# Operands of a B attention job loaded in halves of four heads, five steps ahead of their use

## The chip, the core and the metric

The kernel runs on one core of a Trainium2 chip. Its engines are TensorE (PE, with its weight loads shown as PEld), VectorE (DVE), ScalarE (ACT), GpSimd (POOL) and SyncE (SP), which in this kernel issues every DMA. Each engine works through its own list of instructions in order and waits on semaphores. The metric is the device time of one execution in microseconds (us), taken as the median of several runs; the profile is one more execution, recorded by the hardware.

## What is computed

Two attention blocks over the same 2048 x 512 input are mixed by a gate. Block A goes through 64 segments of 32 tokens in order; each segment attends to itself and to 8 memory rows, and its output gives the memory of the next segment. Block B has 32 heads of width 16 and four blocks of 512 tokens; inside a block it is causal softmax attention, and from the second block on a linear-attention memory of the earlier blocks is added.

```python
# A, segment s: h = [mem, x_s]; 32 heads of 128
q, k, v = h @ Wq, h @ Wk, h @ Wv
p = softmax(q k^T * 128**-0.5 + mask);  o = (p v) @ Wo
mem = o[:8];  outs.append(o[8:])
# B, block s of 512 tokens, 32 heads of 16
p = softmax(qs ks^T * 16**-0.5 + causal);  a_dot = p vs
a_mem = (phi(qs) M) / (phi(qs) z + 1e-6)
o = g * a_mem + (1 - g) * a_dot
M += phi(ks)^T vs;  z += sum(phi(ks))
out = gate * A + (1 - gate) * (B @ wo)
```

## The kernel before, in words

**Recording.** `build` records operations engine by engine through `Prog.op` and `Prog.dma`. Each names what it reads and writes, and from that the waits are derived: an operation waits for the last writer of what it reads, and one that overwrites something waits for all its readers. `emit` writes the lists out in the recorded order, so the place of a call in the Python code is the place of its instructions on each engine. All DMAs of this part stand on SP's one list, in order.

**First stage (to about 90 us).** The projections of B are computed and stored to scratch memory in HBM (`kTd`, `qTd`, `vd`, `pQd`, `mzd`), while the weights of A are loaded.

**Main stage.** `plan_a` goes through the 64 segments of A. For each it runs the units of `A_ORDER` (L822): projections K, Q, V (L855), transposes (L864), scores (S), sums (M), normalising (N), P V (PV), output product (W, L1115) and the memory for the next segment (WT, L1136). Work of B is put between as filler: `bS` and `bP` are one step of B's scores and of B's P V each, `bT` runs one piece of what is waiting in the list `late`. In a segment `bS` stands three times: at its start, and twice near its end, with W1 and one filler between these two. Some 57 of the 64 segments carry steps of B.

**Jobs, halves, steps of B.** A job is 8 heads of one block; there are 16. Step n belongs to job n // 10, to half G = (n // 5) % 2 (four heads) and to k = n % 5. Half G uses partitions 64 G to 64 G + 63 of `KTj` and `QTj`, and the 68 columns from 68 G of `Vj` and `MZj`. In the trace the five steps of a half differ by their shapes on L704: 512 columns x2 for k = 0 and 1, the 384 and 128 columns x4 for k = 2 and 3, 256 columns x4 for k = 4.

**The operands.** There is one buffer of each operand. `load(job, "k")` issues nine DMAs: eight 16-row pieces of `KTj` and one of `QTj`. `load(job, "v")` issues one of `Vj` and, from the second block on (12 of the 16 jobs), one each of `pQj` and `MZj`. The load "k" of the next job is recorded at the end of the tenth `bS` of a job (L708), and waits until that `bS` has read the buffers. The next `bS` (k = 0 of the next job) waits for this load. The load "v" of the next job is recorded in `chain` for G = 1 (L786), after the last P V of the job and after `bN`, which is the product of `pQj` and `MZj` (L779). If `bP` of a new job comes before that, it runs the waiting pieces first (L734).

**What `chain` and `finish` do.** `chain` divides by the softmax sum and adds the memory part, for one half; `finish` transposes the 8 heads' rows (`bT`, L812), and stores them.

Of the kernel before, what the change touches and what calls it, by code (L numbers as in the profile page):

```python
# [216 lines left out]
def bass_gated_mix__memory_aug_recurrent_mem_tr__memory_aug_infini_attn__prompt_kernel(  # L217
    nc, A_x, A_mem0, A_Wq, A_Wk, A_Wv, A_Wo, A_seg_len, B_x, B_wq, B_wk, B_wv, B_wo, B_beta, gate_w, out, dbg=None,
):
    with ExitStack() as es:  # L220
        build(nc, es, A_x, A_mem0, A_Wq, A_Wk, A_Wv, A_Wo, B_wq, B_wk, B_wv, B_wo, B_beta, gate_w, out, dbg)


def build(nc, es, A_x, A_mem0, A_Wq, A_Wk, A_Wv, A_Wo, B_wq, B_wk, B_wv, B_wo, B_beta, gate_w, out, dbg=None):
    v = NS()
# [83 lines left out]
    G = {}  # L309
# [19 lines left out]
    bat = v.bat = BAttn(v)  # L329
# [11 lines left out]
    while len(weights) > 4:  # L341
        weights.pop(0)()
    for part in "kv":
        bat.load(0, part)
    while weights:
        weights.pop(0)()

# [291 lines left out]
class BAttn:  # L639
# [11 lines left out]
        self.obk = None  # L651
        self.jobs_done = 0

    def load(self, job, part):

        v, P, Rs = self.v, self.v.P, self.v.Rs
        if job >= 16 or (job, part) in self.loaded:
            return
        self.loaded.add((job, part))
        sb, f = job // 4, job % 4  # L660
        g, res = P.group("j%s%d" % (part, job), "j" + part), Rs("j" + part.upper())

        def ld(dst, src, reads, name):
            P.dma(g, lambda s: s.dma_start(dst, src), reads=reads, writes=[res], name=name, scratch=True)  # L664
        if part == "k":
            for e in range(2):
                for t in range(4):
                    o = 32 * t + 16 * e
                    ld(v.KTj[e][o:o + 16, :], v.kTd[sb, f, o:o + 16, :], [Rs("kTd%d_%d" % (sb, f)), Rs("KTz")], "ldk%d_%d%d" % (job, e, t))
            ld(v.QTj[:, :], v.qTd[sb, f], [Rs("qTd%d_%d" % (sb, f))], "ldq%d" % job)  # L670
            return
        ld(v.Vj[:, :, :], v.vd[sb, :, :, 136 * f:136 * (f + 1)], [Rs("vd%d_%d" % (sb, tt)) for tt in range(4)], "ldv%d" % job)
        if sb > 0:
            ld(v.pQj[:, :], v.pQd[sb, f], [Rs("pQd%d_%d" % (sb, f))], "ldp%d" % job)
            ld(v.MZj[:, :], v.mzd[sb, :, 136 * f:136 * (f + 1)], [Rs("mzd%d" % sb)], "ldm%d" % job)

    def scores(self):
        v, P, Rs = self.v, self.v.P, self.v.Rs
        n = self.n
        self.n += 1  # L680
        job, G, k = n // 10, (n // 5) % 2, n % 5
        self.load(job, "k")
        bks = v.BK.pair()
        if k < 2:
            mms = [(k, 0, 0, 512, 0)]
            blocks = [(k, 0, q, 128 * q) for q in range(4)]
            diag = [0]
        elif k < 4:
            mms = [(k - 2, 1, 128, 384, 0), (k - 2, 3, 384, 128, 384)]
            blocks = [(k - 2, 1, q, 128 * (q - 1)) for q in (1, 2, 3)] + [(k - 2, 3, 3, 384)]  # L690
            diag = [0, 384]
        else:
            mms = [(e, 2, 256, 256, 256 * e) for e in range(2)]
            blocks = [(e, 2, q, 256 * e + 128 * (q - 2)) for e in range(2) for q in (2, 3)]
            diag = [0, 256]
        self.blocks[n] = blocks
        QT, KT = v.QTj, v.KTj

        def f(pe):
            ins = None  # L700
            for e, kc, q0, w, o in mms:
                for x in range(2):
                    r = slice(64 * G + 32 * x, 64 * G + 32 * x + 32)
                    ins = pe.matmul(v.pb[bks[x]][:, o:o + w], KT[e][r, 128 * kc:128 * (kc + 1)], QT[r, q0:q0 + w], start=True, stop=True,  # L704
                                    tile_position=(r.start, 0))
            return ins
        P.op("pe", f, reads=[Rs("jK")], writes=[v.rbank[b] for b in bks], name="bS%d" % n)
        if n % 10 == 9:  # L708
            self.load(job + 1, "k")
        pt = v.PT[n % 2]  # L710
        rp = Rs("PT%d" % (n % 2))
        P.op("act", lambda a: a.activation(pt[:, :, :], v.ps[:, bks[0]:bks[1] + 1, :], ACT.Exp, scale=v.SCALE_B),  # L712
             reads=[v.rbank[b] for b in bks], writes=[rp], name="bE%d" % n)
        v.BK.give(*bks)
        if k == 4:
            views = [pt[:, :, :].rearrange("p x (d t) -> p (x d) t", t=256)[:, :, 0:128]]
        else:
            views = [pt[:, :, o:o + 128] for o in diag]
        for mv in views:
            P.op("gp", lambda g, mv=mv: g.affine_select(mv, mv, [[0, mv.shape[1]], [1, 128]], ALU.is_ge, 0.0, base=0, channel_multiplier=-1),  # L720
                 reads=[rp], writes=[rp], name="bM%d" % n)
# [6 lines left out]
    def pv(self):  # L728
        v, P, Rs = self.v, self.v.P, self.v.Rs
        n = self.pv_n  # L730
        self.pv_n += 1
        job, G, k = n // 10, (n // 5) % 2, n % 5
        sb, f = job // 4, job % 4
        while self.late and (job, "v") not in self.loaded:  # L734
            self.run_late(1)
        self.load(job, "v")
        if k == 0:
            self.obk = v.BK.take(long=True)
        ob = self.obk
        pt, V = v.PT[n % 2], v.Vj  # L740
        blocks = self.blocks.pop(n)

        def fpv(pe):
            ins = None
            first = k == 0
            for e, kc, q, col in blocks:
                for x in range(2):
                    hh = 2 * x + e
                    o = 17 * (4 * q + hh)
                    h = 4 * G + hh  # L750
                    ins = pe.matmul(v.pb[ob][:, o:o + 17], pt[:, x, col:col + 128], V[:, kc, 17 * h:17 * (h + 1)], start=first, stop=True,  # L751
                                    skip_group_check=True)
                    first = False
            return ins
        P.op("pe", fpv, reads=[Rs("PT%d" % (n % 2)), Rs("jV")], writes=[v.rbank[ob]], name="bP%d" % n)
        if k == 4:
            self.late.append(lambda: self.chain(job, G, ob))
            if G == 1:
                self.late.append(lambda: self.finish(sb, f))

    def chain(self, job, G, ob):
        v, P, Rs = self.v, self.v.P, self.v.Rs
        sb, f = job // 4, job % 4
        h0 = 8 * f + 4 * G
        nm = "%d_%d%d" % (sb, f, G)
        T1 = v.pb[ob][:, 0:272].rearrange("p (q h w) -> p q h w", q=4, h=4)
        dst = v.orow[:, :, 64 * G:64 * (G + 1)].rearrange("p q (h d) -> p q h d", h=4)
# [4 lines left out]
        nb = None  # L772
        if sb:
            nb = v.BK.take()

            def fn(pe):
                ins = None
                for q in range(4):
                    ins = pe.matmul(v.pb[nb][:, 68 * q:68 * (q + 1)], v.pQj[:, 128 * q:128 * (q + 1)], v.MZj[:, 68 * G:68 * (G + 1)],  # L779
                                    start=True, stop=True)  # L780
                return ins
            P.op("pe", fn, reads=[Rs("jV")], writes=[v.rbank[nb]], name="bN" + nm)
            T2 = v.pb[nb][:, 0:272].rearrange("p (q h w) -> p q h w", q=4, h=4)
        P.op("dve", lambda d: d.reciprocal(rd, T1[:, :, :, 16]), reads=[v.rbank[ob], rr], writes=[rr], name="brd" + nm)
        P.op("dve", lambda d: d.tensor_tensor(rd, rd, bc(v.omgB_sb), ALU.mult), reads=[rr, Rs("omgB")], writes=[rr], name="brg" + nm)
        if G == 1:  # L786
            self.load(job + 1, "v")
        if not sb:
            P.op("dve", lambda d: d.tensor_tensor(dst, T1[:, :, :, 0:16], up(rd), ALU.mult), reads=[v.rbank[ob], rr], writes=[ro], name="bo" + nm)
            v.BK.give(ob)  # L790
# [38 lines left out]
def plan_a(v, nseg):  # L829
# [163 lines left out]
    def segment(s, fill):  # L993
# [179 lines left out]
        for b in range(2):  # L1173
            for m in "KQV":
                units["%s%d" % (m, b)] = lambda m=m, b=b: nat_pass(m, b, ENG["%s%d" % (m, b)])
            for m in "KQ":
                units["T%s%d" % (m, b)] = lambda m=m, b=b: tr(m, b, ENG["T%s%d" % (m, b)])
            units["S%d" % b] = lambda b=b: scores(b)
            units["M%d" % b] = lambda b=b: sums(b)
            units["N%d" % b] = lambda b=b: norm(b)  # L1180
            units["PV%d" % b] = lambda b=b: held.__setitem__(b, pv(b))
            units["W%d" % b] = lambda b=b: wo(b)
            for half in range(2):
                units["E%d%s" % (b, "ab"[half])] = lambda b=b, half=half: out_ev(b, half)
# [74 lines left out]
```

## Time and profile before

| what | value |
|---|---|
| median of 3 runs | 1195.66 us |
| the profiled execution, its time | 1193.82 us |
| its span, first to last instruction | 1192.1 us (1.7 us of its time lie around the span) |
| PE busy | 1026.2 us (86%) |
| ACT busy | 671.2 us (56%) |
| DVE busy | 513.3 us (43%) |
| POOL busy | 212.5 us (18%) |
| mean granted clock of TensorE | 0.959 of full speed |

Busy time is an average over stages; waits are read from the views that say what ended them. The granted clock is 1.00 (2.4 GHz) or 0.50 (1.2 GHz) at any moment, a window shows the mean.

### The profile page before, as it was taken

What the parts mean: (1) busy time and instruction counts of PE and PEld (TensorE: products, weight loads), DVE (VectorE), ACT (ScalarE), POOL (GpSimd) and SP (SyncE); (2) the same over time, 40 slices, a digit from 0 to 9 for tenths busy, and PEclk for the clock granted to TensorE, in tenths of its full rate; (3) what the DMA queues carried; (4) which work ended last, traced back from release to release, by engine and by line L of the source; (5) the groups of instructions that cost most, each with busy time, mean ns of one, the idle gap of its engine ahead of it and who ended that gap; (6) DMA issues with size and microseconds to landing.
All of it is one profiled execution on the core that took longest, in us unless ns stands there. A gap on an engine that the chain in (4) does not pass through costs nothing.

```text
span 1192.1 us, 54216 instructions
## 1 busy us (share of the span) xinstructions
PE 1026.2 (86%) x24389; PEld 553.3 (46%) x24389; DVE 513.3 (43%) x1309; ACT 671.2 (56%) x1371; POOL 212.5 (18%) x544
## 2 busy tenths in 40 slices
PE   8968997899789799979998999698978899999874
PEld 4424544454445455444554555354534455554432
DVE  4643443344335444444444444243433444444432
ACT  4435665566546566656665666365645656655442
POOL 6101111111112121211122121121211121220000
PEclk9989999899989899999999999899989999999997
DMA  8894000000011101010101010000010001000001
GB/s 270 272 319 145 13 12 12 17 12 17 12 26 34 31 17 31 8 26 3 41 21 44 4 39 8 25 8 22 28 32 17 16 22 30 18 8 21 26 3 32
DMA packets 55551, 51.79 MB, mean 43 GB/s; under 512 B 23696, under 2 KB 53784, under 8 KB 53784
## 3 DMA queue, kind: packets, MB, share of 16 engines
q1 hardware_dynamic: 55320, 48.32, 13.4%
q8 instruction: 192, 3.15, 1.1%
q14 instruction: 39, 0.32, 0.1%
HBM read 33.60 MB, written 14.70 MB: 41 GB/s over the span
## 4 chain that ended last, share of the span: by engine, by line
PE 73%; ACT 9%; DVE 7%; DMA 5%; SPq 3%; issue 3%; POOL 1%; ACTq 0%; POOLq 0%; DVEq 0%
PE ps L855 35%; PE ps L1115 8%; PE ps L864 6%; PE ps L704 4%; SPq L664 3%; PE ps L751 3%; PE ps L583 2%; ACT PT L712 2%; PE ps L558 2%; DVE Pn_sb L1064 2%; PE ps L1078 2%; DMA QTj<-scr_qTd 2%; PE ps L918 2%; PE ps L964 1%; ACT R_sb L1057 1%
## 5 line engine op out<-in xcount | busy, mean ns | idle before, releaser
L712 ACT ACTIVATE PT<-ps 128x1024 bf16<-128x1024 f32 x160 | 163.3, 1022 | 99.1 <-PE ps L704 95.3
L855 PE MATMUL ps<-Wk_sb,hT 128*32 128x512 bf16 x2048 | 142.5, 401 | 0.7 <-DVE hT L1142 0.6
L720 POOL TENSOR_SCALAR_AFFINE_SELECT PT<-PT 128x256 bf16<-128x256 bf16 (+1 forms) x224 | 98.4, 439 | 223.8 <-ACT PT L712 215.3
L855 PE MATMUL ps<-Wq_sb,hT 128*32 128x512 bf16 x2048 | 137.1, 389 | 0.0
L855 PE MATMUL ps<-Wv_sb,hT 128*32 128x512 bf16 x2048 | 135.5, 383 | 1.6 <-DVE amem L801 0.9
L1115 PE MATMUL ps<-Wo_sb,OT_sb 128*32 128x512 bf16 x2048 | 134.5, 384 | 1.7 <-DMA Wo_sb<-in_A_Wo_dram 1.7
L1169 POOL COPY OTL<-OT_sb 128x256 bf16<-128x256 bf16 x64 | 25.4, 397 | 545.3 <-DVE OT_sb L321 432.9
L1125 DVE TENSOR_TENSOR aW_sb<-ps,aW_sb 128x256 bf16<-128x256 f32 x128 | 48.4, 420 | 152.3 <-ACT aW_sb L319 152.3
L319 ACT ACTIVATE KN_sb<-ps 128x512 bf16<-128x512 f32 x64 | 38.2, 597 | 128.7 <-PE ps L855 128.7
L704 PE MATMUL ps<-QTj,KTj 32*128 32x384 bf16 (+3 forms) x512 | 64.8, 310 | 41.5 <-DMA QTj<-scr_qTd 40.5
L319 ACT ACTIVATE OT_sb<-ps 128x320 bf16<-128x320 f32 x192 | 75.9, 429 | 19.6 <-PE ps L1087 19.0
L855 PEld LDWEIGHTS ps<-Wq_sb,hT 128*32 128x32 bf16 x2048 | 56.1, 100 | 60.9 <-issue 6.8
L855 PEld LDWEIGHTS ps<-Wk_sb,hT 128*32 128x32 bf16 x2048 | 50.5, 100 | 62.9 <-issue 16.0
L321 DVE CAST KN_sb<-ps 128x512 bf16<-128x512 f32 x64 | 44.2, 691 | 80.8 <-PE ps L855 80.6
L1057 ACT ACTIVATE R_sb<-ps 128x160 f32<-128x160 f32 x128 | 38.9, 304 | 69.6 <-PE ps L1053 69.6
L1078 PE MATMUL ps<-Pn_sb,V_sb 32*128 32x40 bf16 x2048 | 36.4, 178 | 44.5 <-DVE Pn_sb L1068 39.1
L751 PEld LDWEIGHTS ps<-Vj,PT 128*128 128x128 bf16 x1280 | 44.5, 96 | 55.7 <-issue 39.4
L751 PE MATMUL ps<-Vj,PT 128*128 128x17 bf16 x1280 | 57.4, 172 | 14.9 <-DMA MZj<-scr_mzd 10.6
L321 DVE COPY QT_sb<-ps 128x512 bf16<-128x512 bf16 x64 | 27.2, 425 | 99.5 <-PE ps L864 99.5
L1064 DVE TENSOR_TENSOR Pn_sb<-P_sb,R_sb 128x160 bf16<-128x160 bf16 x128 | 44.1, 345 | 51.0 <-ACT R_sb L1060 42.2
L1115 PEld LDWEIGHTS ps<-Wo_sb,OT_sb 128*32 128x32 bf16 x2048 | 43.4, 96 | 46.8 <-issue 14.9
L855 PEld LDWEIGHTS ps<-Wv_sb,hT 128*32 128x32 bf16 x2048 | 46.1, 95 | 35.0 <-ACT R_sb L1057 1.5
(136 smaller groups left out, 1827.1 us busy)
## 6 DMA issues: line engine op xcount, KB each, us to landing
Wk_sb<-in_A_Wk_dram SPq DMA_DIRECT2D x4, 1024.0 KB, 6.7
Wq_sb<-in_A_Wq_dram SPq DMA_DIRECT2D x4, 1024.0 KB, 7.0
Wv_sb<-in_A_Wv_dram SPq DMA_DIRECT2D x4, 1024.0 KB, 8.1
Wo_sb<-in_A_Wo_dram SPq DMA_DIRECT2D x4, 1024.0 KB, 11.6
scr_vd<-V SPq DMA_DIRECT2D x16, 136.0 KB, 5.1
Vj<-scr_vd SPq DMA_DIRECT2D x16, 136.0 KB, 2.7
Wo_sb<-in_A_x_dram SPq DMA_DIRECT2D x4, 512.0 KB, 8.1
scr_kTd<-stgk SPq DMA_DIRECT2D x16, 128.0 KB, 6.1
```

Of the source, the lines that this page charges most:

```text
L319: P.op("act", lambda a: a.activation(dst, src, ACT.Copy), reads=[v.rbank[k] for k in bks], writes=dres, name=name)
L321: P.op("dve", lambda d: d.tensor_copy(dst, src), reads=[v.rbank[k] for k in bks], writes=dres, name=name)
L704: ins = pe.matmul(v.pb[bks[x]][:, o:o + w], KT[e][r, 128 * kc:128 * (kc + 1)], QT[r, q0:q0 + w], start=True, stop=True, tile_position=(r.s ...
L712: P.op("act", lambda a: a.activation(pt[:, :, :], v.ps[:, bks[0]:bks[1] + 1, :], ACT.Exp, scale=v.SCALE_B), reads=[v.rbank[b] for b in bks ...
L720: P.op("gp", lambda g, mv=mv: g.affine_select(mv, mv, [[0, mv.shape[1]], [1, 128]], ALU.is_ge, 0.0, base=0, channel_multiplier=-1), reads= ...
L751: ins = pe.matmul(v.pb[ob][:, o:o + 17], pt[:, x, col:col + 128], V[:, kc, 17 * h:17 * (h + 1)], start=first, stop=True, skip_group_check= ...
L855: ins = pe.matmul(pb[bk][SEG * j:SEG * (j + 1), :], lhs(c), w_sb[:, c, n0:n0 + 512], start=(c == 0), stop=(c == C - 1))
L864: ins = pe.transpose(pb16[bk][:, i * 128:(i + 1) * 128], nat[:, b, i * 128:(i + 1) * 128], ident[:, :])
L1057: P.op("act", lambda a: a.activation(R_sb[:, b, :], pb[bk][:, 224:384], ACT.Ln), reads=[rbank[bk]], writes=[Rs("R%d" % b)], name="ln%d_%d" ...
L1064: P.op("dve", lambda d: d.tensor_tensor(wide(Pn_sb, b)[:, :, 0:L], wide(P_sb, b)[:, :, 0:L], R_sb[:, b, :].rearrange("p (i q) -> p i q", q ...
L1078: ins = pe.matmul(pb[bks[j]][:, L * i:L * (i + 1)], V_sb[SEG * j:SEG * (j + 1), b, i * E:(i + 1) * E], Pn_sb[SEG * j:SEG * (j + 1), b, LW ...
L1115: ins = pe.matmul(pb[bk][SEG * j:SEG * (j + 1), :], OT_sb[:, h, 0:SEG], Wo_sb[:, h, :], start=(b == 0 and i == 0), stop=(b == 1 and i == 3))
```

## The change

Every load is split by half: part "k" into four pieces of `KTj` and 64 rows of `QTj`, part "v" into 68 columns of `Vj` and `MZj` and 64 rows of `pQj`. Each half has its own name for dependencies (`jK0`, `jK1`, `jV0`, `jV1`), so a `bS` or `bP` waits for its half alone. The half G of the next job is recorded when the fifth step of that half of this job is recorded (k = 4), or, for part "v", in `chain` of that half. `bN` reads all 128 rows of `pQj`, so it now waits for both halves of part "v", of which one may already belong to the next job; the columns of `MZj` that it uses are zero in the other half's rows.

```diff
     for part in "kv":
-        bat.load(0, part)
+        for G in range(2):
+            bat.load(0, G, part)
...
-    def load(self, job, part):
+    def load(self, job, G, part):
...
-        g, res = P.group("j%s%d" % (part, job), "j" + part), Rs("j" + part.upper())
+        g, res = P.group("j%s%d_%d" % (part, job, G), "j%s%d" % (part, G)), Rs("j%s%d" % (part.upper(), G))
+        rows, cols = slice(64 * G, 64 * G + 64), slice(68 * G, 68 * G + 68)
...
         if part == "k":
             for e in range(2):
-                for t in range(4):
+                for t in (2 * G, 2 * G + 1):
                     o = 32 * t + 16 * e
...
-            ld(v.QTj[:, :], v.qTd[sb, f], [Rs("qTd%d_%d" % (sb, f))], "ldq%d" % job)
+            ld(v.QTj[rows, :], v.qTd[sb, f, rows, :], [Rs("qTd%d_%d" % (sb, f))], "ldq")
             return
...
+        o = 136 * f + 68 * G
+        ld(v.Vj[:, :, cols], v.vd[sb, :, :, o:o + 68], [Rs("vd%d_%d" % (sb, tt)) for tt in range(4)], "ldv")
         if sb > 0:
...
+            ld(v.pQj[rows, :], v.pQd[sb, f, rows, :], [Rs("pQd%d_%d" % (sb, f))], "ldp")
+            ld(v.MZj[:, cols], v.mzd[sb, :, o:o + 68], [Rs("mzd%d" % sb)], "ldm")
...
-        P.op("pe", f, reads=[Rs("jK")], writes=[v.rbank[b] for b in bks], name="bS%d" % n)
-        if n % 10 == 9:
-            self.load(job + 1, "k")
+        P.op("pe", f, reads=[Rs("jK%d" % G)], writes=[v.rbank[b] for b in bks], name="bS%d" % n)
+        if k == 4:
+            self.load(job + 1, G, "k")
...
-        while self.late and (job, "v") not in self.loaded:
+        while self.late and (job, G, "v") not in self.loaded:
             self.run_late(1)
-        self.load(job, "v")
+        self.load(job, G, "v")
...
-            P.op("pe", fn, reads=[Rs("jV")], writes=[v.rbank[nb]], name="bN" + nm)
+            P.op("pe", fn, reads=[Rs("jV0"), Rs("jV1")], writes=[v.rbank[nb]], name="bN" + nm)
...
-        if G == 1:
-            self.load(job + 1, "v")
+        self.load(job + 1, G, "v")
```

On SP, the loads of job 2 (the first three rows) and of job 3 stand in the kernel before with a store of finished rows of B (L817) and one of A (L945) between them:

```order
L664 DMA KTj<-scr_kTd 16x512 x8
L664 DMA QTj<-scr_qTd 128x512
L664 DMA Vj<-scr_vd 128x4x136
L817 DMA scr_oTd<-oTs 128x512
L945 DMA scr_aTd<-aT_st 128x512
L664 DMA KTj<-scr_kTd 16x512 x8
L664 DMA QTj<-scr_qTd 128x512
L664 DMA Vj<-scr_vd 128x4x136
```

In the changed kernel (its lines 667, 820 and 948 are lines 664, 817 and 945 of before) the two halves of job 2 are these, with the same two stores behind the second:

```order
L667 DMA KTj<-scr_kTd 16x512 x4
L667 DMA QTj<-scr_qTd 64x512
L667 DMA Vj<-scr_vd 128x4x68
L667 DMA KTj<-scr_kTd 16x512 x4
L667 DMA QTj<-scr_qTd 64x512
L667 DMA Vj<-scr_vd 128x4x68
L948 DMA scr_aTd<-aT_st 128x512
L820 DMA scr_oTd<-oTs 128x512
```

Each half's group of DMAs stands on SP's list where five steps of the other half of the same buffers are still to run, and the job's loads are 10 and 2 (or 6) DMAs in place of 9 and 1 (or 3).

On PE, the list of before has the transposes of a finished job, L812, directly behind the first `bP` of the next job (L751) and ahead of the scores of A, L1023, at four places (jobs 2, 4, 11 and 13; this is the first):

```order
L751 MATMUL ps<-Vj,PT 128x17 x8
L864 MATMUL ps<-ident,QN_sb 128x128 x4
L751 MATMUL ps<-Vj,PT 128x17 x8
L812 MATMUL ps<-ident,orow 128x128 x4
L1023 MATMUL ps<-mneg,ident 32x224 x4
```

In the changed kernel they stand (as L815) at the end of that segment, behind WT (L1139) and ahead of the next `bS` (L708):

```order
L1139 MATMUL ps<-selL,aW_sb 128x32 x8
L939 MATMUL ps<-selL,LN_sb 128x32 x8
L815 MATMUL ps<-ident,orow 128x128 x4
L708 MATMUL ps<-QTj,KTj 128x384 x2
```

Those four moves, two of which also move the `bN` (L779) behind the `bP` beside it, are all that moves on PE; ACT and POOL keep their order, and DVE moves the copies of the four transposes with them.

## Rows read from the trace of the kernel before

**Rows 1.** The page: span, busy time by engine, granted clock by slices.
```profile
span 1192.1 us, 54216 instructions
PE 1026.2 (86%) x24389; PEld 553.3 (46%) x24389; DVE 513.3 (43%) x1309; ACT 671.2 (56%) x1371; POOL 212.5 (18%) x544
PEclk9989999899989899999999999899989999999997
```

**Rows 2.** Groups by line: busy, mean ns | idle before, what ended it.
```profile
L704 PE MATMUL ps<-QTj,KTj 32*128 32x384 bf16 (+3 forms) x512 | 64.8, 310 | 41.5 <-DMA QTj<-scr_qTd 40.5 <-ACT PT L712 0.3
L751 PE MATMUL ps<-Vj,PT 128*128 128x17 bf16 x1280 | 57.4, 172 | 14.9 <-DMA MZj<-scr_mzd 10.6 <-DMA Vj<-scr_vd 2.6 <-POOL PT L720 1.5
```

**Rows 3.** The line of the loads (L664): who waited for it (us, times).
```profile
  PE ps L704: 40.5, 9
  PE ps L751: 13.2, 4
```

**Rows 4.** Timeline of PE, end of segment 6 to segment 7: start, us, instruction [idle <-releaser].
```profile
202.23 0.58 PE L1136 MATMUL ps<-selL,aW_sb 128*128 128x32 bf16 x8
207.93 0.61 PE L704 MATMUL ps<-QTj,KTj 32*128 32x512 bf16 x2 [5.12 <-DMA QTj<-scr_qTd]
208.47 1.90 PE L855 MATMUL ps<-Wk_sb,hT 128*32 128x512 bf16 x16
211.59 1.03 PE L855 MATMUL ps<-Wk_sb,hT 128*32 128x512 bf16 x16
...
218.43 0.36 PE L751 MATMUL ps<-Vj,PT 128*128 128x17 bf16 x8 [2.65 <-DMA Vj<-scr_vd]
```

**Rows 5.** Timeline of SP's list at the same place, and at one later load.
```profile
202.08 3.56 SPq L664 DMA_DIRECT2D KTj<-scr_kTd  x8
205.68 0.42 SPq L664 DMA_DIRECT2D QTj<-scr_qTd  x1
...
453.27 0.34 SPq L986 DMA_DIRECT2D out_dram<-aTg  x1
453.71 3.37 SPq L664 DMA_DIRECT2D KTj<-scr_kTd  x5
```

**Rows 6.** Windows with a load wait: window, us, busy by engine, PEclk, DMA.
```profile
321.60:349.30 27.70, 18.77 (x387) 9.53 (x383) 7.74 (x21) 10.44 (x22) 2.51 (x6) 0.75 0.14 36
935.60:972.50 36.90, 30.88 (x772) 17.08 (x770) 15.72 (x42) 21.13 (x43) 6.74 (x16) 0.95 0.10 25
sum 281.10, PE 213.74 PEld 112.79 DVE 101.69 ACT 134.00 POOL 41.42; mean PE 23.75 PEld 12.53 DVE 11.30 ACT 14.89 POOL 4.60
```

**Rows 7.** Windows between them, without such a wait, same columns.
```profile
110.20:202.20 92.00, 84.15 (x2218) 46.47 (x2215) 40.07 (x104) 60.38 (x123) 17.51 (x44) 1.00 0.04 9
842.90:875.90 33.00, 31.26 (x777) 16.98 (x774) 15.64 (x41) 21.71 (x45) 7.04 (x17) 1.00 0.10 27
sum 676.30, PE 627.41 PEld 345.17 DVE 309.83 ACT 439.00 POOL 136.51; mean PE 62.74 PEld 34.52 DVE 30.98 ACT 43.90 POOL 13.65
```

**Rows 8.** Windows inside segment 7: the wait, and the time after it.
```profile
204.50:211.30 6.80, 3.37 (x30) 1.21 (x34) 0.69 (x1) 1.02 (x1) 0.67 (x2) 0.50 0.14 33
211.30:218.10 6.80, 4.48 (x80) 2.25 (x72) 2.30 (x6) 2.80 (x5) 0.00 (x0) 1.00 0.10 20
218.10:221.60 3.50, 3.17 (x76) 1.98 (x80) 0.42 (x1) 0.36 (x1) 0.00 (x0) 0.51 0.12 40
```

**Rows 9.** Loads by tile: issue ns on SP, min/median/max, and time to landing (QTj, Vj).
```profile
L664 SPq DMA_DIRECT2D KTj<-scr_kTd x128: 303/420/1567, 82.3 to 1010.3; - x128
L664 SPq DMA_DIRECT2D QTj<-scr_qTd x16: 416/421/431, 86.5 to 1010.8; - x16
DMA to landing us min/median/max: 2.0/2.1/5.1
L664 SPq DMA_DIRECT2D Vj<-scr_vd x16: 529/530/612, 86.9 to 1011.8; - x16
DMA to landing us min/median/max: 2.6/2.7/5.0
```

**Rows 10.** Timeline of PE: a step k = 4, the next job's k = 0; `bN` of both halves.
```profile
123.01 0.39 PE L704 MATMUL ps<-QTj,KTj 32*128 32x256 bf16 x4
153.33 0.39 PE L704 MATMUL ps<-QTj,KTj 32*128 32x512 bf16 x2
668.09 0.29 PE L779 MATMUL ps<-MZj,pQj 128*128 128x68 bf16 x4
689.78 0.28 PE L779 MATMUL ps<-MZj,pQj 128*128 128x68 bf16 x4
```

**Rows 11.** Timeline around the first job: SP's loads, PE's wait for `Wo_sb`.
```profile
87.60 8.03 SPq L448 DMA_DIRECT2D Wo_sb<-in_A_Wo_dram  x4
104.94 1.40 PE L1115 MATMUL ps<-Wo_sb,OT_sb 128*32 128x512 bf16 x16 [1.73 <-DMA Wo_sb<-in_A_Wo_dram]
```

More of the change, by code (lines that the diff above doesn't have):

```diff
@@ L652, in __init__ @@
         self.jobs_done = 0
-    def load(self, job, part):
+    def load(self, job, G, part):
         v, P, Rs = self.v, self.v.P, self.v.Rs
-        if job >= 16 or (job, part) in self.loaded:
+        if job >= 16 or (job, G, part) in self.loaded:
             return
-        self.loaded.add((job, part))
+        self.loaded.add((job, G, part))
         sb, f = job // 4, job % 4
-        g, res = P.group("j%s%d" % (part, job), "j" + part), Rs("j" + part.upper())
+        g, res = P.group("j%s%d_%d" % (part, job, G), "j%s%d" % (part, G)), Rs("j%s%d" % (part.upper(), G))
+        rows, cols = slice(64 * G, 64 * G + 64), slice(68 * G, 68 * G + 68)
         def ld(dst, src, reads, name):
-            P.dma(g, lambda s: s.dma_start(dst, src), reads=reads, writes=[res], name=name, scratch=True)
+            P.dma(g, lambda s: s.dma_start(dst, src), reads=reads, writes=[res], name="%s%d_%d" % (name, job, G), scratch=True)
         if part == "k":
             for e in range(2):
-                for t in range(4):
+                for t in (2 * G, 2 * G + 1):
                     o = 32 * t + 16 * e
-                    ld(v.KTj[e][o:o + 16, :], v.kTd[sb, f, o:o + 16, :], [Rs("kTd%d_%d" % (sb, f)), Rs("KTz")], "ldk%d_%d%d" % (job, e, t))
-            ld(v.QTj[:, :], v.qTd[sb, f], [Rs("qTd%d_%d" % (sb, f))], "ldq%d" % job)
+                    ld(v.KTj[e][o:o + 16, :], v.kTd[sb, f, o:o + 16, :], [Rs("kTd%d_%d" % (sb, f)), Rs("KTz")], "ldk")
+            ld(v.QTj[rows, :], v.qTd[sb, f, rows, :], [Rs("qTd%d_%d" % (sb, f))], "ldq")
             return
-        ld(v.Vj[:, :, :], v.vd[sb, :, :, 136 * f:136 * (f + 1)], [Rs("vd%d_%d" % (sb, tt)) for tt in range(4)], "ldv%d" % job)
+        o = 136 * f + 68 * G
+        ld(v.Vj[:, :, cols], v.vd[sb, :, :, o:o + 68], [Rs("vd%d_%d" % (sb, tt)) for tt in range(4)], "ldv")
         if sb > 0:
-            ld(v.pQj[:, :], v.pQd[sb, f], [Rs("pQd%d_%d" % (sb, f))], "ldp%d" % job)
-            ld(v.MZj[:, :], v.mzd[sb, :, 136 * f:136 * (f + 1)], [Rs("mzd%d" % sb)], "ldm%d" % job)
+            ld(v.pQj[rows, :], v.pQd[sb, f, rows, :], [Rs("pQd%d_%d" % (sb, f))], "ldp")
+            ld(v.MZj[:, cols], v.mzd[sb, :, o:o + 68], [Rs("mzd%d" % sb)], "ldm")
     def scores(self):
@@ L681, in scores @@
         job, G, k = n // 10, (n // 5) % 2, n % 5
-        self.load(job, "k")
+        self.load(job, G, "k")
         bks = v.BK.pair()
@@ L754, in fpv @@
             return ins
-        P.op("pe", fpv, reads=[Rs("PT%d" % (n % 2)), Rs("jV")], writes=[v.rbank[ob]], name="bP%d" % n)
+        P.op("pe", fpv, reads=[Rs("PT%d" % (n % 2)), Rs("jV%d" % G)], writes=[v.rbank[ob]], name="bP%d" % n)
         if k == 4:
```

## The prediction

> **What bounds the kernel now.** I read first the page [rows 1]. PE is busy for 86% of the span, no other engine for more than 56%, so PE's own list sets the pace, and the question is when PE stands still or runs slow. The row of the clock has an 8 in six of its 40 slices where the others have a 9: something repeats that slows TensorE. The groups by line say what [rows 2]: PE stood idle 41.5 us ahead of B's scores (L704), of which 40.5 us were ended by a load of QTj, and 14.9 us ahead of B's P V (L751), of which 10.6 + 2.6 us were ended by loads of MZj and Vj. The view of line L664, from which these loads come, has the count: 9 waits of the scores and 4 of P V [rows 3]. Together 40.5 + 13.2 = **53.7 us**.
>
> The timeline shows one of the nine [rows 4, 5]. SP can start on the next job's KTj only when the tenth step has been read, at 202.08; it takes about 4 us to issue nine DMAs one after the other, the last lands 2 us later, and the next step, which stands only one P V and WT further on PE's list, waits from about 202.8 to 207.93. All of A's next segment stands behind it. In six more of the 15 changes of job a segment or its longer part lies between the two steps, and PE doesn't wait. In the same segment P V of the new job waits once more, for a load of Vj that could only be recorded just ahead of it.
>
> A wait costs more than its own length. In the 6.8 us window around its end the granted clock is 0.50, that is 1.2 GHz in place of 2.4 [rows 8]; the sixteen matmuls of a projection take 1.90 us there and 1.03 us after it [rows 4]. So I cut the main stage, from WT of segment 0 (110.2) to WT of segment 56 (1067.6), into nine stretches with such waits and the ten between them. The nine hold 13 segments and last 281.1 us, their clocks 0.75 to 0.95 [rows 6]. The ten hold 43 segments and last 676.3 us, and the clock of each is 1.00 [rows 7].
>
> **The change part by part.** *The waits and the slow time behind them.* An undisturbed segment takes 676.3 / 43 = 15.73 us. Thirteen would take 204.5 us and took 281.1: **76.6 us** are lost to load waits and what follows them. Of this 53.7 us are the waits, so 22.9 us are work at the lower clock. That this is the right size: in the nine stretches length times (1 - clock) adds up to 33 us, and some 10 of these fall into the waits themselves, where nothing runs. For the bounds I take the quickest undisturbed stretch, 92.0 / 6 = 15.33 us a segment, which gives 281.1 - 199.3 = 81.8, and the slowest, 33.0 / 2 = 16.5, which gives 66.6. I take 76.6, since the 13 segments lie at all four places in the groups of four.
>
> *Whether the halves come in time.* Part "k" of half G is now wanted six steps after the step that frees it. The closest such pair before is 123.01 to 153.33 [rows 10], 30 us. What a half takes isn't in the trace: four KTj and one QTj, by the rows of the wholes 5 x 0.42 = 2.1 us to issue [rows 9], or 5 x 0.67 = 3.4 at the slowest pace of a group that is shown [rows 5]; the landing between QTj's 2.0 and 5.1 us. That is 4.1 to 8.5 us of 30. Part "v" is closest at `bN`: half 0 of the next job is recorded right behind `bN` of half 0 and wanted by `bN` of half 1, because that reads all of pQj; 668.09 to 689.78 is 21.7 us [rows 10]. It needs three issues of about half a microsecond and a landing of at most Vj's 5.0 us [rows 9]: 6.6 us. If the cover were gone, PE would wait these 6.6 us at `bN`, A's scores of that segment stand behind it, and DVE's division behind both.
>
> *SP's list.* The DMAs of the loads go from 16 x 9 + 4 + 12 x 3 = 184 to 16 x 10 + 4 x 2 + 12 x 6 = 240. The 56 more, at 0.42 to 0.53 us each [rows 9], are 24 to 30 us on an engine that mostly waits; nothing of PE's list waits for them. A load could stand behind another entry that waits. But every such entry was recorded earlier, so what it waits for runs earlier on PE too: at 453.27 the load stood behind an output store and was let go 0.4 us after it [rows 5]. With a whole group ahead of it a half is late by 3 or 4 us, of 21.7. Cost zero.
>
> *More waits to decode.* PE has some 50 more semaphore waits, of which nearly all are met when they are reached. In the rows of L704 only 41.5 - 40.5 = 1.0 us of idle time has another cause than the loads, over all 160 steps, six met changes of job among them [rows 2]; so between 0 and 1 us. I take 0.
>
> *The four moved transposes.* They go from ahead of A's scores to behind WT, where they stand at most of the other 12 changes of job, whose segments are among the undisturbed ones. Zero, and at most the 0.6 us that one takes, either way, times four.
>
> *The first job.* Its loads stand on SP's list ahead of the four loads of Wo_sb [rows 11]. One QTj and one Vj more are 0.42 + 0.53 = 0.95 us [rows 9], and PE already waits 1.73 us for Wo_sb [rows 11]. So **1.0 us lost**; at best nothing, if not the issue but the transfer sets the landing.
>
> *A rule that speaks against it.* QTj's 128 rows landed in 2.1 us and a 16-row piece of KTj took the same 0.42 us to issue [rows 9], so I don't expect a half to be cheaper than a whole. The Trainium skill (DMA: Bandwidth & Descriptors, Rules for kernel authors) says of two transfers to disjoint partition halves "Don't bother": they share the same engines and serialize, one transfer over 128 partitions is to be preferred. By it alone the split buys nothing, and with the 24 to 30 us of issues added the time would be about 1220. The rows agree on the price and decide otherwise on the sum, since here the split moves the transfer away from its use.
>
> **The sum.** 1193.8 (the profiled execution) - 76.6 + 1.0 = 1118.2. The median of the runs is 1.8 above the profiled one, so **1120.0 us**.
>
> **The rivals.**
> *The clock doesn't come back.* If the low clock has another cause than the waits, only the idle time returns: 1195.7 - 53.7 + 1.0 = 1143. For it: nothing but its presence in single windows. Against it: it is 1.00 in all ten stretches without waits [rows 7]. 4%.
> *The halves cost as much as wholes and stay in view.* This is the mechanism behind the rule above: 10 and 6 DMAs in two portions. A whole part "k" takes about 4.0 + 2.1 = 6.1 us, two halves 2 x (2.1 + 2.1) = 8.4; 16 jobs with 2.3 us more, and half of the old wait exposed at some of them, leave about 40 us: 1160. Against it are the 30 and 21.7 us of cover. 3%.
> *The change doesn't do what it says for "k".* The loads are recorded early but SP reaches them late, behind stores that wait for work of A. Then the nine long waits stay and only the four of P V go, 13.2 us and some 6 of slow clock: 1176. For it: SP has one list. Against it: the order above, in which no entry waits for something recorded later. 2%.
> *Slower.* `bN` now depends on the next job's half. There are 24 of them, and the change loses when each waits more than 76.6 / 24 = 3.2 us; that is when a half of part "v" is let go so late that it lands 21.7 + 3.2 = 24.9 us after its record. With no cover at all, 24 x 6.6 = 158 us of new waits, 1195.7 - 76.6 + 158 = 1277. Nothing in the landing times (at most 5.1 us) speaks for it. 3%.
>
> **How the numbers follow.** The likeliest case has 88%. Its own range comes from the quickest and slowest segments and the first job: 1195.7 - 81.8 = 1113.9 to 1195.7 - 66.6 + 1.0 + 1.0 = 1131.1. I widen it below by 2 us for the transposes, and give 1112 to 1132; the rivals' 12% lie outside. A measurement of this kernel can tell about 2%, 24 us: faster below 1171.8. Likeliest case, clock and halves are faster: 95%. The rival in which "k" stays is within 2%: 2%. Slower: 3%.
>
> **What the changed profile would show.** No row of L708 or L755 (the scores and P V of the changed kernel) with idle time ended by a load; the clock 1.00 from 110 us to the end of B's steps; WT to WT never more than 17 us in that time; 240 issues on the line of the loads; the wait for Wo_sb longer by about 1 us. The argument is wrong if segments of over 20 us are left, if the clock falls without a wait ahead of it, or if `bN` (L782) waits for a DMA.

## The result and the profile after

The changed kernel takes 1120.24 us (median of 4 runs, 1118.31 to 1122.67), the kernel before 1195.41 us beside it. The ratio is 0.938, with a 95% interval of 0.935 to 0.941; it leaves out one of the four runs of the kernel before, which took 1680.55 us. Two more measurements of the same program gave 0.9386 and 0.9368. The forecast was 1120.

| what | before | after |
|---|---|---|
| median | 1195.41 us | 1120.24 us |
| span of the profiled execution | 1192.1 us | 1121.0 us |
| PE busy | 1026.2 us (86%) | 1006.3 us (90%) |
| PE idle ahead of B's scores | 41.5 us | 1.1 us |
| PE idle ahead of B's P V | 14.9 us | 1.7 us |
| mean granted clock | 0.959 | 0.983 |

The page of the changed kernel, in the lines of [rows 1]:

```profile
span 1121.0 us, 54313 instructions
PE 1006.3 (90%) x24389; PEld 547.4 (49%) x24389; DVE 511.8 (46%) x1309; ACT 670.3 (60%) x1371; POOL 212.2 (19%) x544
PEclk9988999999999999999999999999999999999997
```

PE does the same 24389 matmuls in 20 us less busy time, because fewer of them run at 1.2 GHz; the 8s in the middle of the clock row are gone. The groups by line show what became of the waits (L708 and L755 are L704 and L751 of before, the answer to [rows 2]):

```profile
L708 PE MATMUL ps<-QTj,KTj 32*128 32x384 bf16 (+3 forms) x512 | 62.9, 303 | 1.1 <-ACT PT L716 0.2
L755 PE MATMUL ps<-Vj,PT 128*128 128x17 bf16 x1280 | 57.3, 172 | 1.7 <-POOL PT L724 1.5
```

In these two rows no idle time is ended by a DMA any more. The timeline of PE at the place of [rows 4], from WT of segment 6 on (L1139):

```profile
201.84 0.58 PE L1139 MATMUL ps<-selL,aW_sb 128*128 128x32 bf16 x8
202.36 0.39 PE L708 MATMUL ps<-QTj,KTj 32*128 32x512 bf16 x2
202.71 1.05 PE L858 MATMUL ps<-Wk_sb,hT 128*32 128x512 bf16 x16
...
217.30 0.58 PE L1139 MATMUL ps<-selL,aW_sb 128*128 128x32 bf16 x8
218.30 0.35 PE L939 MATMUL ps<-selL,LN_sb 128*128 128x32 bf16 x8 [0.42 <-DVE hT L1145]
218.50 0.38 PE L815 MATMUL ps<-ident,orow 128*128 128x128 bf16 x4
```

The new job's first scores follow WT at once, the projection behind them takes 1.05 us and not 1.90, and segment 7 lasts 217.30 - 201.84 = 15.5 us, where it lasted 26.2. The transposes of the finished job stand behind WT.

A half of `QTj` or of `Vj` costs about what the whole cost, as the rows by tile show (issue on SP in ns, then landing; QTj with 64 rows, Vj with 68 columns; [rows 9] has the wholes):

```profile
L667 SPq DMA_DIRECT2D QTj<-scr_qTd x32: 450/464/1677, 81.9 to 938.0; - x32
DMA to landing us min/median/max: 2.0/2.1/6.0
L667 SPq DMA_DIRECT2D Vj<-scr_vd x32: 526/558/630, 85.0 to 940.0; - x32
DMA to landing us min/median/max: 2.3/2.5/4.3
```

### The profile page after: what moved, and what is told of

It is laid out like the page before. It is cut to its first block, busy times and chain, and to the rows that moved or that the text cites. A ratio compares the mean times of both kernels' runs of the same rounds, so it can differ in the third digit from the quotient of the medians.

```text
span 1121.0 us, 54313 instructions
## 1 busy us (share of the span) xinstructions
PE 1006.3 (90%) x24389; PEld 547.4 (49%) x24389; DVE 511.8 (46%) x1309; ACT 670.3 (60%) x1371; POOL 212.2 (19%) x544
## 4 chain that ended last, share of the span: by engine, by line
PE 76%; ACT 9%; DVE 8%; DMA 3%; issue 3%; SPq 0%; POOL 0%; ACTq 0%; DVEq 0%; POOLq 0%
PE ps L858 37%; PE ps L1118 10%; PE ps L867 6%; PE ps L708 4%; ACT PT L716 3%; PE ps L755 3%; PE ps L584 2%; DVE Pn_sb L1067 2%; PE ps L921 2%; PE ps L967 2%; PE ps L1081 2%; PE ps L559 1%; PE ps L1139 1%; DMA scr_pQd<-stgp 1%; ACT R_sb L1060 1%
## 5 line engine op out<-in xcount | busy, mean ns | idle before, releaser
L1118 PE MATMUL ps<-Wo_sb,OT_sb 128*32 128x512 bf16 x2048 | 137.3, 391 | 3.3 <-DMA Wo_sb<-in_A_Wo_dram 3.3
L858 PE MATMUL ps<-Wk_sb,hT 128*32 128x512 bf16 x2048 | 134.3, 382 | 0.8 <-DVE hT L1145 0.6
L858 PE MATMUL ps<-Wq_sb,hT 128*32 128x512 bf16 x2048 | 133.6, 381 | 0.0
L755 PEld LDWEIGHTS ps<-Vj,PT 128*128 128x128 bf16 x1280 | 44.4, 96 | 41.7 <-issue 28.4
L708 PE MATMUL ps<-QTj,KTj 32*128 32x384 bf16 (+3 forms) x512 | 62.9, 303 | 1.1 <-ACT PT L716 0.2
L319 ACT ACTIVATE V_sb<-ps 128x512 bf16<-128x512 f32 x64 | 38.2, 597 | 42.8 <-PE ps L858 42.8
```

The lines of the kernel that those rows point to most:

```text
L319: P.op("act", lambda a: a.activation(dst, src, ACT.Copy), reads=[v.rbank[k] for k in bks], writes=dres, name=name)
L858: ins = pe.matmul(pb[bk][SEG * j:SEG * (j + 1), :], lhs(c), w_sb[:, c, n0:n0 + 512], start=(c == 0), stop=(c == C - 1))
L1118: ins = pe.matmul(pb[bk][SEG * j:SEG * (j + 1), :], OT_sb[:, h, 0:SEG], Wo_sb[:, h, :], start=(b == 0 and i == 0), stop=(b == 1 and i == 3))
```

## The experiments

Seven questions were put to the chip: do the two parts add up, is it the split or the freedom to start that counts, how much lead is needed, does the slow clock come from the waits, what are the four moved transposes worth, what does the start cost, and does the first profile's odd clock repeat.

### One part at a time

Part "k" alone as changed, part "v" loaded whole as before (only the core of the diff against the changed kernel):

```diff
     def load(self, job, G, part):
+        G = 0 if part == "v" else G
...
-        self.load(job + 1, G, "v")
+        if G == 1:
+            self.load(job + 1, 0, "v")
```

> Only part 'k' (KTj, QTj) is loaded in halves and early; part 'v' is loaded whole, recorded in chain of the second half, as before. Theory (each load wait costs its length and the slow clock behind it, independently of the others): the nine waits of the scores are gone, the four of P V stay with 13.2 us of idle time and some 15 us at half clock behind them, about 7 us: 1120.2 + 20 = 1140 us. Rival (removed waits come back as longer waits elsewhere, so parts don't add up): the four waits of P V grow well beyond 13 us and the time is over 1150 us.

Measured: 1138.21 us, ratio 0.954 (0.952 to 0.956). The rows of the loads' line say who waited:

```profile
  PE ps L755: 13.5, 4
```

Four waits of P V, 13.5 us in all, each within 0.3 us of its length before. And part "v" alone, with "k" loaded whole after the tenth step:

```diff
     def load(self, job, G, part):
+        G = 0 if part == "k" else G
...
-        if k == 4:
-            self.load(job + 1, G, "k")
+        if n % 10 == 9:
+            self.load(job + 1, 0, "k")
```

> Only part 'v' (Vj, pQj, MZj) is loaded in halves and early; part 'k' is loaded whole after the tenth step, as before. Theory (costs add): nine waits of the scores stay at about 40 us, the four of P V are gone, 1195.4 - 20 = 1175 us; together with the run with 'k' alone the two gains (55 and 20) make up the 75 us. Rival (parts don't add): less than 10 us gained, because the segments that lost both waits are set by the longer one: over 1185 us.

Measured: 1178.70 us, ratio 0.987 (0.985 to 0.989). Nine waits of the scores are left:

```profile
  PE ps L708: 39.6, 9
```

By the ratios "k" is worth 55 us and "v" 16 us (13 to 18), together 71 of the 73 to 75 that both bring. The parts add, within the intervals; no wait came back elsewhere. The 20 us expected for "v" were a little too many.

### The split without the early record

```diff
-        if k == 4:
-            self.load(job + 1, G, "k")
+        if n % 10 == 9:
+            for g in range(2):
+                self.load(job + 1, g, "k")
...
-        self.load(job + 1, G, "v")
+        if G == 1:
+            for g in range(2):
+                self.load(job + 1, g, "v")
```

> The loads are split in the same halves, but both halves of the next job are recorded where the whole was before: 'k' after the tenth step, 'v' in chain of the second half. Theory (the gain is the early place, not the split): the first half needs 4 KTj and one QTj, 2.2 us of issue and 2.1 us of landing, in place of 6.1 us, so the nine waits shrink by about 1.9 us each, 17 us; the four of P V stay at about 13 us; the clock still falls: 1195.4 - 17 = 1178 us, down to 1165 if some of the shorter waits leave the clock up. Rival (smaller transfers are the gain): under 1145 us. The Trainium skill (DMA: Bandwidth & Descriptors, Rules for kernel authors) would have two transfers to disjoint halves serialize with no gain: 1195 us or more.

Measured: 1131.14 us, ratio 0.949 (0.945 to 0.952). The expectation was wrong by over 30 us, and the rival's side was right on the number but not on the reason. The timeline of SP's list has the answer:

```profile
170.38 1.70 SPq L667 DMA_DIRECT2D KTj<-scr_kTd  x4
172.12 0.48 SPq L667 DMA_DIRECT2D QTj<-scr_qTd  x1
201.27 1.69 SPq L667 DMA_DIRECT2D KTj<-scr_kTd  x4
203.00 0.47 SPq L667 DMA_DIRECT2D QTj<-scr_qTd  x1
```

The first two rows are half 0 of job 2, whose use is at 201.94. They are recorded behind the tenth step of job 1, which PE runs at 200.85, and yet they start at 170.38, right behind the last step of half 0 (169.95 on PE's timeline). The place of the record only says what stands ahead of a load on SP's list. The load starts when these entries are through and its own semaphores are met, and half 0's load names half 0 alone. For part "k", what makes the load early is the separate name more than the separate place. The place still counts for something: by the same two timelines the loads "k" of half 0 of eight jobs (5 to 9 and 13 to 15) stand behind other entries and start 18 to 34 us after their half is free, yet still 10 us or more ahead of their use.

What is left of the waits is this, on PE's timeline:

```profile
718.74 0.34 PE L756 MATMUL ps<-Vj,PT 128*128 128x17 bf16 x8 [3.51 <-DMA MZj<-scr_mzd]
835.76 0.35 PE L756 MATMUL ps<-Vj,PT 128*128 128x17 bf16 x8 [3.49 <-DMA MZj<-scr_mzd]
```

Two waits of part "v", of jobs 11 and 13, both in the blocks where `bN` exists. The load of half 0 is recorded here behind `bN` of the second half, which reads all of `pQj`, and a load waits for the readers recorded ahead of it. In the changed kernel it is recorded ahead of that `bN`. For part "v", then, the place of the record does count.

### The split, tied to the old release

To see the split without its freedom, every half load of that kernel also waits for the last operation recorded on PE:

```diff
+        last = P.ops["pe"][-1:] if job else []
...
-            P.dma(g, lambda s: s.dma_start(dst, src), reads=reads, writes=[res], name="%s%d_%d" % (name, job, G), scratch=True)
+            P.dma(g, lambda s: s.dma_start(dst, src), reads=reads, writes=[res], deps=last, name="%s%d_%d" % (name, job, G), scratch=True)
```

> The kernel of halves_late, in which every half load in addition waits for the last operation recorded on PE at that place: 'k' for the tenth step of the job, 'v' for the product bN or P V of the second half. So the transfers are split, but no half may start before the whole could. New theory (halves_late was fast because half 0 was free to start as soon as its own last reader was done, wherever its load is recorded): now the waits are back, the first half of 'k' needs 2.2 us of issue and 2.1 of landing after the tenth step in place of 6.0, nine waits of some 2.8 us, 25 us; the four of P V stay at about 13 us; 1195.4 - 16 = 1179 us, down to 1164 if the clock stays up behind the shorter waits. Rival (smaller transfers as such bring the gain): about 1131 us, as halves_late.

Measured: 1182.28 us, ratio 0.985 (0.979 to 0.991), by the ratio 1177 on the scale of 1195.4. The rows of the loads' line:

```profile
  PE ps L709: 22.8, 9
  PE ps L757: 13.1, 4
```

Nine waits of 2.5 us on average in place of 4.5 [rows 3], and the four of P V unchanged. Smaller transfers alone are worth 18 us, 11 to 26 by the interval. The other 57 need the early start, and some 8 of them also the new place of the four transposes, which this kernel has at the old one (see below). Here the Trainium skill's rule (DMA: Bandwidth & Descriptors, Rules for kernel authors), that two transfers to disjoint partition halves are not worth making because they serialize, is half borne out. On SP's timeline the issue of half 1 of job 2 does follow that of half 0 (`KTj` from 205.02 and from 207.28 us). But PE needs only half 0 to go on, and does so at 208.92 us, before `QTj` of half 1 is issued at 209.29. Whether the transfers themselves serialize isn't shown by this run.

### Half 0 freed of `bN`

If the reader decides, then the two waits left in the late version come from `bN` of the second half, which reads all of `pQj`. So it was given its own 64 rows:

```diff
-                    ins = pe.matmul(v.pb[nb][:, 68 * q:68 * (q + 1)], v.pQj[:, 128 * q:128 * (q + 1)], v.MZj[:, 68 * G:68 * (G + 1)],
-                                    start=True, stop=True)
+                    ins = pe.matmul(v.pb[nb][:, 68 * q:68 * (q + 1)], v.pQj[hr, 128 * q:128 * (q + 1)], v.MZj[hr, 68 * G:68 * (G + 1)],
+                                    start=True, stop=True, tile_position=(64 * G, 0))
...
-            P.op("pe", fn, reads=[Rs("jV0"), Rs("jV1")], writes=[v.rbank[nb]], name="bN" + nm)
+            P.op("pe", fn, reads=[Rs("jV%d" % G)], writes=[v.rbank[nb]], name="bN" + nm)
```

> The kernel of halves_late, in which bN uses only its own half's 64 rows of pQj and MZj (the other half's rows are multiplied with zeros) and waits for its own half of part 'v' alone. In halves_late two waits of 3.5 us for MZj are left, at jobs 11 and 13, with 3.4 us at half clock behind each. New theory (half 0 of part 'v' was held until bN of the second half, because that read it; the reader decides, not the place of the load): both waits are gone and the time is that of the changed kernel, 1121 us, within 2. Rival (the place of the load in chain of the second half holds it up): the two waits stay, 1131 us.

Measured: 1128.67 us, ratio 0.942 (0.939 to 0.945). No PE instruction waits for a load of B's operands any more, as the theory said, but the time didn't follow. PE's timeline at the same two places:

```profile
714.30 0.36 PE L756 MATMUL ps<-Vj,PT 128*128 128x17 bf16 x8
716.98 0.38 PE L819 MATMUL ps<-ident,orow 128*128 128x128 bf16 x4 [2.32 <-POOL orow L810]
...
832.56 0.38 PE L819 MATMUL ps<-ident,orow 128*128 128x128 bf16 x4 [2.32 <-POOL orow L810]
```

In this kernel the transposes `bT` still stand directly behind `bN` and P V, and wait for DVE and POOL to finish the rows that they transpose. That the wait for the load had hidden this one is what the next run tests.

### The four moved transposes put back

This was tested on the changed kernel itself, with all loads early and PE's list that of the kernel before:

```diff
-        while self.late and (job, G, "v") not in self.loaded:
+        while self.late and ((job, G, "v") not in self.loaded or (n % 10 == 0 and len(self.late) > 1)):
```

> The changed kernel with the four transposes (bT) put back ahead of A's scores, so that PE's list is that of the kernel before; all loads stay halved and early. Theory from late_own (the wait for the load covered the time that DVE and GpSimd need between bN and the transposes): PE waits about 2.3 us for the rows at jobs 11 and 13 and 0.6 us at jobs 2 and 4, with some 3.4 us at half clock behind the first two: 5.8 + 2 to 3 us, 1121 + 8 = 1129 us. Rival (the four moves cost and gain nothing, as predicted): 1121 us, no wait at the transposes.

Measured: 1128.07 us, ratio 0.944 (0.940 to 0.948); the changed kernel beside it took 1119.18 us, ratio 0.937 (0.933 to 0.941). PE's timeline, idle time ahead of the transposes at the four places:

```profile
213.14 0.40 PE L815 MATMUL ps<-ident,orow 128*128 128x128 bf16 x4 [0.60 <-DVE orow L792]
323.42 0.40 PE L815 MATMUL ps<-ident,orow 128*128 128x128 bf16 x4 [0.60 <-DVE orow L792]
721.48 0.38 PE L815 MATMUL ps<-ident,orow 128*128 128x128 bf16 x4 [2.53 <-POOL orow L806]
835.90 0.59 PE L815 MATMUL ps<-ident,orow 128*128 128x128 bf16 x4 [2.53 <-POOL orow L806]
```

These are 6.3 us of idle time, and behind the last one some 3.4 us at half clock. From WT of segment 0 to WT of segment 56 this kernel takes 1004.07 - 113.21 = 890.9 us, and the changed one beside it 993.38 - 110.81 = 882.6. So the move (of the transposes, and at two of the places of `bN`) is worth about 8 us, which the prediction had put at zero. In the kernel before, PE's timeline at job 11 has the wait for the load, and the transposes behind it wait for nothing:

```profile
764.72 0.36 PE L751 MATMUL ps<-Vj,PT 128*128 128x17 bf16 x8 [3.73 <-DMA MZj<-scr_mzd]
764.94 0.59 PE L812 MATMUL ps<-ident,orow 128*128 128x128 bf16 x4
```

### Two steps of lead

```diff
-        if k == 4:
-            self.load(job + 1, G, "k")
+        if k == 3 and n > 5:
+            self.load(job + G, 1 - G, "k")
```

> The changed kernel with the half loads of part 'k' recorded at step k = 3 of the other half, two steps ahead of use instead of six; part 'v' unchanged. In the changed kernel's trace the time from such a step to the use is 2.9 to 3.6 us at nine of the 30 places and over 12 us at the others. Theory (a half needs 2.2 us of issue and 2.1 us of landing, 4.3 us, and all cover beyond that is worth nothing): nine waits of about 1 us, clock mostly up, 1120 + 10 = 1130 us, up to 1140 if the clock falls behind some of them. Rival (a half needs the upper bound, 8.5 us): nine waits of about 5 us with slow clock, over 1175 us. Rival (the distance matters for another reason, such as SP's list): waits at the places with 12 us too.

Measured: 1121.53 us, ratio 0.938 (0.935 to 0.941), the same as the changed kernel beside it (0.9386). No wait for a load of B's operands is left. The expectation rested on the same error as the one for the late halves: that the place of the record is the time of the start. SP's timeline for the load "k" of half 1 of job 2, in the changed kernel (first row) and in this one:

```profile
201.69 1.70 SPq L667 DMA_DIRECT2D KTj<-scr_kTd  x4
...
222.13 0.43 SPq L820 DMA_DIRECT2D scr_oTd<-oTs  x1
222.61 2.65 SPq L667 DMA_DIRECT2D KTj<-scr_kTd  x4
```

The load does start later here, by 21 us, directly behind a store that stands ahead of it on the list; but its use is at 235.80, another 13 us later. From job 1 on, the loads "k" start 11 to 28 us ahead of their use in this kernel and 29 to 44 us ahead in the changed one, and a half needs about 4.3 (2.2 to issue and 2.1 to land). So none came late, and how little lead would do stays open.

### The waits filled with matmuls

The kernel before, with bursts of matmuls ahead of the 13 waiting operations:

```diff
+FILL_S = {20: 22, 40: 20, 50: 21, 70: 20, 90: 11, 110: 21, 120: 18, 130: 20, 140: 17}
+FILL_P = {20: 10, 40: 13, 110: 15, 130: 14}
...
+                ins = pe.matmul(v.pb[bks[0]], v.ident[:, :], v.woB_sb[:, i % 4, :], start=True, stop=True)
...
+        self.fill(FILL_S.get(n), bks)
         P.op("pe", f, reads=[Rs("jK")], writes=[v.rbank[b] for b in bks], name="bS%d" % n)
```

> The kernel before, with 128x512 matmuls into banks that are overwritten next put ahead of the 13 operations that wait for a load, as many as take up about each wait (9 bursts of 11 to 22, 4 of 10 to 15, 0.216 us each at full clock). The loads stay late. Theory (the slow clock behind a wait comes from TensorE's idle time): the clock stays at 1.00 through the main stage, the idle time is merely filled, and only the 22.9 us come back: 1172.5 us, between 1168 and 1180 if a burst is off by some tenths of a us. Rival (the clock falls for another reason, such as the transfer or the change of job): clock below 1 in the same stretches and 1195 us or more.

Measured: 1174.50 us, ratio 0.984 (0.981 to 0.987), 16 to 22 us gained with every load as late as before. PE still waits 6.2 us for the loads, in short pieces. One window over the main stage has the clock that the theory asked for, and none of its 56 segments, read one by one, has a mean below 0.99:

```profile
110.00:1050.00 940.00, 870.93 (x21370) 472.66 (x21362) 411.23 (x1080) 573.61 (x1164) 177.78 (x427) 1.00 0.08 21
```

So the slow clock came with TensorE's idle time, not with the change of job or the transfer, and it was worth about 20 us of the 75.

### The start

```diff
     for part in "kv":
-        for G in range(2):
-            bat.load(0, G, part)
+        bat.load(0, 0, part)
     while weights:
         weights.pop(0)()
+    for part in "kv":
+        bat.load(0, 1, part)
```

> The changed kernel with the second halves of job 0's loads (4 KTj, QTj, Vj) recorded behind the four loads of Wo_sb instead of ahead of them. In the changed kernel's trace these six issues take 3.0 us, and PE waits 3.3 us for Wo_sb at 103.5 us with 6.8 us at half clock from 102.9. Theory (Wo_sb lands when SP issues it): the wait is 0.3 us, and 3 to 6 us are gained: 1114 to 1117 us. Rival (the transfer of 4 MB, not the issue, sets the landing): the wait stays near 3 us and the time at 1120 us.

Measured: 1118.56 us, ratio 0.9367 (0.9339 to 0.9394), against 0.9386 (0.9358 to 0.9413) for the changed kernel beside it. The intervals overlap, so a gain isn't shown. The wait itself differs from one execution of the same program to the next: in three profiles of the changed kernel it was 3.3, 1.2 and 2.9 us, here 1.0.

```profile
L1118 PE MATMUL ps<-Wo_sb,OT_sb 128*32 128x512 bf16 x2048 | 137.3, 391 | 3.3 <-DMA Wo_sb<-in_A_Wo_dram 3.3
L1118 PE MATMUL ps<-Wo_sb,OT_sb 128*32 128x512 bf16 x2048 | 134.8, 385 | 1.2 <-DMA Wo_sb<-in_A_Wo_dram 1.2
```

(The first row is of the profile after, the second of its first repetition.) This is the only version that might beat the changed kernel, and it stays open whether it does.

### The changed kernel again

> The changed kernel once more, beside the next two on one chip. All theories: 1120 us within 2. Its first profile has two falls of the clock to 0.50, at 529.5 and 546.6 us, with no load wait ahead of them. If they belong to the place in the program, they are at the same segments (27 and 28) again; if they are a matter of chance, elsewhere or nowhere, and the main stage from WT of segment 0 to WT of segment 56 is about 4 us shorter, 882 us.

Measured: 1121.14 us. 

> The changed kernel beside it on the same chip: 1121 us within 2. A third profile of the same program shows whether the clock falls anywhere between 110 and 996 us without a wait for a load: in the first it did twice, in the second not.

Measured: 1119.18 us. In neither profile does the clock fall between 110 us and the end of B's steps. This is read segment by segment: over the whole stage the mean rounds to 1.00 in the profile after as well, in spite of its two falls. The windows of the main stage, from WT of segment 0 to WT of segment 56, in the first repetition (one window) and in the profile after (three):

```profile
110.90:993.60 882.70, 820.09 (x21136) 452.06 (x21133) 410.51 (x1080) 572.29 (x1163) 177.80 (x427) 1.00 0.09 22
```

```profile
110.10:515.90 405.80, 375.96 (x9764) 207.28 (x9760) 184.49 (x480) 263.94 (x538) 78.97 (x193) 1.00 0.08 20
515.90:551.80 35.90, 32.07 (x763) 16.64 (x760) 15.77 (x45) 20.28 (x42) 7.36 (x17) 0.90 0.10 22
551.80:996.00 444.20, 414.50 (x10620) 228.60 (x10618) 210.15 (x556) 287.92 (x585) 91.47 (x217) 1.00 0.10 24
```

The two falls of the first profile lie in its second window, segments 27 and 28, which last 17.61 and 18.15 us there and 15.4 and 16.5 us in both repetitions. So the program alone doesn't decide. But the place isn't chance either. In the kernel with the halves tied (`halves_tied`) the same two segments have a granted clock of 0.90 and 0.91 and, from WT (L1143) to WT, the same lengths of 17.61 and 18.15 us, again with no load wait in them:

```profile
549.16 0.58 PE L1143 MATMUL ps<-selL,aW_sb 128*128 128x32 bf16 x8
562.87 1.90 PE L1122 MATMUL ps<-Wo_sb,OT_sb 128*32 128x512 bf16 x16
566.77 0.35 PE L1143 MATMUL ps<-selL,aW_sb 128*128 128x32 bf16 x8
584.92 0.58 PE L1143 MATMUL ps<-selL,aW_sb 128*128 128x32 bf16 x8
```

## Why the prediction was right, point by point

**The waits and the clock: right, and right in size.** The main stage was 957.4 us long between these two points and is 882.7 us in a profile without odd falls of the clock: 74.7 us less, against a term of 76.6. A segment takes 882.7 / 56 = 15.76 us, against the 15.73 read from the undisturbed stretches [rows 7]. In the first profile it is 885.9 us, 3 us more, which the two falls explain. The split into idle time and slow clock holds too: filling the waits brought 16 to 22 us, a little under the 22.9. But two signs that the prediction named went against it in the first profile: the clock fell twice without a load wait ahead of it, and segments of 17.6 and 18.2 us are over its limit of 17. So the load waits aren't the only cause of a slow clock; the others cost 3 us there, against the 75.

**In time: right.** No half came late, and a half cost about what a whole costs. For part "k" the prediction counted the cover from the step that frees the half, 30 us at the closest; in the trace after, the loads from job 1 on start 0.4 to 2.4 us behind the start of that step and at least 29 us ahead of their use. What it didn't tell apart is the name and the place: the expectations for the late halves and for the two steps of lead took the place of the record for the start, and failed on that. A load starts when the readers of what it names are done, those recorded ahead of it, and when the entries ahead of it on SP's list are through. With the names kept and all records late, 62 of the 75 us are still there; with the release tied together again, 18.

**The four moved transposes: this step failed.** The prediction gave them "Zero, and at most the 0.6 us that one takes, either way, times four". They are worth about 8 us, because at their old place they would have waited 2.5 us twice and 0.6 us twice for DVE and POOL. Before, the wait for the load of the next job stood just ahead of them and covered this, and the trace of before showed no wait at that line. The sum came out right all the same: the 15.73 us of an undisturbed segment already have the transposes behind WT. With PE's list left as it was, the time is 1128 us, 8 above the forecast and within its range.

**SP's list, the extra waits on PE: right.** The 56 more DMAs cost nothing that shows; L708 has 1.1 us of idle time in all.

**The start: not decided.** The predicted 1.0 us is smaller than what the wait for Wo_sb varies by between executions.

**The rivals.** The clock came back; the halves are about as dear as wholes, but out of view; `bN` waits for nothing. That a half is no cheaper doesn't decide here, since what the halves buy is the earlier start.

Not tried: whole loads into a second set of buffers, which could start early without a split. Whether there is room for the set beside the tiles of the main stage isn't shown here.

## What to carry to other kernels

A load that waits for its buffer starts when the last reader of whatever it is named to overwrite is done and the entries ahead of it on its list are through; give each part that is read apart a name of its own, and look on the DMA queue's timeline for when it starts, not in the code for where it is issued. Price a repeated stall by the length of disturbed and undisturbed stretches of the same work rather than by its idle time alone: here 54 us of waiting went with 75 us of longer stretches, of which some 20 were slow clock. And before calling a wait gone, ask what stood right behind it: a shorter wait may have been hidden under it, and will show once the first is removed.

## What the runs showed of the hardware that was not expected

TensorE's clock fell to 1.2 GHz where PE waited for nothing long, in some executions and not in others of the same program. The windows of the profile after, around the first such place:

```profile
525.90:529.50 3.60, 2.15 (x90) 1.13 (x90) 1.54 (x4) 1.73 (x5) 0.39 (x1) 1.00 0.02 5
529.50:533.00 3.50, 3.50 (x36) 1.08 (x32) 0.76 (x2) 1.68 (x3) 0.82 (x3) 0.51 0.02 5
```

Ahead of the fall PE was busy for 2.15 of 3.6 us, with its longest wait 0.93 us; then two projections ran at half speed. Two such falls lengthened the segments 27 and 28 to 17.6 and 18.2 us. The places recur: the same two segments fell in the kernel with the halves tied, and segment 53 (clock 0.90, without a load wait) both in the kernel with part "k" alone and in the one with Wo_sb first, at 17.7 and 18.0 us. In the three profiles of the changed kernel segment 53 has a clock of 1.00. And the same wait need not have the same effect: of the two waits of 2.53 us in the kernel with the transposes put back, the first left the clock up, the second was followed by half clock:

```profile
718.30:721.70 3.40, 0.87 (x24) 0.79 (x21) 1.89 (x7) 0.97 (x2) 0.72 (x1) 1.00 0.26 45
721.70:725.10 3.40, 3.00 (x127) 1.86 (x125) 1.48 (x4) 1.68 (x6) 0.00 (x0) 1.00 0.14 43
...
832.40:835.80 3.40, 0.96 (x28) 0.82 (x24) 1.88 (x7) 1.12 (x2) 0.72 (x1) 0.99 0.23 40
835.80:839.20 3.40, 3.30 (x84) 1.93 (x88) 0.68 (x2) 0.42 (x2) 0.00 (x0) 0.50 0.18 48
```

What decides between the two isn't shown by these runs.
